# Attention from chunk 2 on in plain float32, the two heads of a unit in halves of the array

## The chip, the cores and the metric

The program runs on one core of one Trainium2 chip. A core has five engines that work at the same time, each in the order of its own instruction list, and that wait for each other by semaphores: TensorE (PE in the profile: matmuls, transposes by an identity; its weight loads are listed apart as PEld), VectorE (DVE), ScalarE (ACT), GpSimd (POOL) and SyncE (SP, which here issues DMAs). The metric is the device time of one execution in microseconds (us), as the median of several runs; lower is better.

## The reference

Three layers follow each other. The sizes are B, H, S, D = 4, 8, 576, 64 (so 2304 tokens of width 512), 2048 hidden columns in the second layer, and 8 experts with 1024 hidden columns in the third.

```python
scores = (q @ k.T) / sqrt(D)                       # per batch and head
scores = where((rel >= 0) & (rel < 128), scores - slope[h] * abs(rel), -1e9)
attn = exp(scores - max); attn = attn / (attn.sum(-1) + 1e-9)
x = attn @ v                                       # (2304, 512)
h = x @ w_in                                       # 2048 wide
x = (h * clip(h + 3, 0, 6) / 6) @ w_out
idx = argmax(cosine(x, expert_emb) / tau)          # one expert per token
out = gate * (relu(x @ w1[idx]) @ w2[idx])
```

A query sees its own key and the 127 before it, so a block of 128 queries needs at most two blocks of 128 keys.

## The kernel before

The 2304 tokens are nine chunks of 256 (c = 0 to 8). A chunk's attention is four **units** of two heads (p = 0 to 3). Chunks 0 and 1 use the class `Early`: loads of whole rows, transposes by PE, plain float32 matmuls, the two heads of a unit side by side in halves of the array (for the scores the upper and the lower 64 rows, for the values the left and the right 64 columns). Chunks 2 to 8 (28 units) use the class `Unit`. The batches end at token 576, 1152 and 1728, so the blocks differ by chunk: in chunks 3, 5 and 8 a unit has two query blocks of 128 with 256 keys each ("even"), in chunk 4 two blocks, one of them without keys before it, and in chunks 2, 6 and 7 three blocks, two of them of 64 queries.

`Unit` before works in float32r with every operand split into a rounded part and a remainder. `split_qk` (L570) casts the keys and the scaled queries on ACT and subtracts on DVE; two DMAs of ACT's queue (L591, L592) then exchange the two halves of the queries' tile into a second tile, q2. `split_v` (L594) splits the values on ACT or POOL. Each head has its own group of score matmuls (L625, two for each block, with all 128 rows), its own softmax (`soften`: DVE adds the table and takes the minimum, L639, joins own and earlier keys, L648 or L654, ACT makes the exponential, L659), `normalise` (DVE makes the reciprocal, L676 and L677, POOL or ACT multiplies, L680 to L690), transposes on PE (L697), `split_p` (ACT cast, DVE remainder by L160, POOL masks both parts, L711 and L715), value matmuls (L742, two for each window of keys), and `gather` (L753, L754), which adds the two halves of the result.

Chunks from 1 on go through the second layer in eight steps each: `gemm1` (L780, 24 matmuls into h_ps), `swish` (ACT relu L790, DVE gate L797), `split_g` (ACT cast gh, remainder gl on POOL or DVE by a table, I_GL), `gemm2` (L823, 12 matmuls into y_ps). `Route` chooses the experts of a finished chunk. The third layer comes after the last chunk.

What sets the order: for chunk 0 and the units of `Early` a planner lists the tasks (its ranks are PIECE_RANK, UNIT_RANK and so on). After it every call has a step number (`at`), and PE runs the calls in the order of these numbers; a step is about 3.7 us. UNITS_2 and UNIT say at which step a unit begins, PARTS the distances inside it, FIRST_1 and FIRST where the steps of the second layer stand. DVE, ACT, POOL and SP are ordered by the scheduler, which starts from the same calls. All PSUM tiles come from one pool of eight banks.

## Time and profile before

| what | value |
|---|---|
| runs | 845.07, 852.41, 852.37 us; median 852.37 us |
| the profiled execution | 850.65 us, its span from first to last instruction 848.9 us |
| PE busy | 809.2 us (95%) in 5404 matmuls |
| DVE, ACT, POOL busy | 551.0, 459.2, 314.5 us |
| mean granted TensorE clock | 0.968 of full speed |

The profile is of one execution. A timeline row gives the start, the length, the engine, the line, the tiles written and read, the shape and the number of merged instructions. The lengths of matmuls overlap, since they are pipelined; the time that PE really spends on a group is the distance from its start to the start of the next group. A plain float32 matmul appears as two instructions, a float32r matmul as one. "Idle before" in brackets is PE's wait and what ended it.

### The profile page before, as it was taken

The page shows a single profiled execution, that of the slowest core. Times are in us where ns is not written, and L with a number is a line of the kernel's source. Part 1 is how long each engine was busy: PE and PEld are TensorE (multiplying, and loading weights), DVE is VectorE, ACT ScalarE, POOL GpSimd, SP SyncE. Part 2 cuts the span into 40 slices and gives each one's busy share as a digit, 9 for nine tenths or more (in the row PEclk, how much of TensorE's full clock was granted, in tenths as well). Part 3 has the DMA queues.
Part 4 walks back from the last instruction along what each step waited for, and adds up shares of the span by engine and source line. Part 5 has one row for each costly group of instructions (what it writes and reads, how often), then busy time and mean ns, then how long its engine had stood idle before and what let it go on. Part 6 is the DMA issues. An engine that isn't in the chain of part 4 may idle for free. (4 is left out here: it accounts for less than half of the span.)

```text
span 848.9 us, 16092 instructions
## 1 busy us (share of the span) xinstructions
PE 809.2 (95%) x5404; PEld 721.3 (85%) x5404; DVE 551.0 (65%) x1482; ACT 459.2 (54%) x1140; POOL 314.5 (37%) x617
## 2 busy tenths in 40 slices
PE   5899989899999999999999999999999999999994
PEld 3666578679989999988899999998899999999993
DVE  4999967575767776867677776324565566447620
ACT  6676657466646566567467565333655445435410
POOL 1000014473544556776557645123233122132300
PEclk8699999899999999999999999999999999999997
DMA  9927133323333233233233221005647655465200
GB/s 263 332 81 221 79 69 67 44 58 80 58 56 83 47 65 81 52 58 72 43 58 86 50 48 29 2 25 165 221 133 239 226 182 197 169 217 177 100 24 26
DMA packets 156664, 90.86 MB, mean 107 GB/s; under 512 B 117491, under 2 KB 134003, under 8 KB 156576
## 3 DMA queue, kind: packets, MB, share of 16 engines
q1 hardware_dynamic: 148352, 72.85, 31.4%
q10 hardware_dynamic: 4480, 7.34, 4.0%
q0 software_dynamic: 3744, 9.58, 3.3%
q8 instruction: 45, 0.74, 0.4%
q14 instruction: 43, 0.35, 0.2%
HBM read 72.76 MB, written 9.74 MB: 97 GB/s over the span
## 5 line engine op out<-in xcount | busy, mean ns | idle before, releaser
L780 PE MATMUL h_ps<-xs,w_i 128*128 128x256 f32 x1536 | 202.3, 289 | 2.0 <-ACT xs L159 2.0
L780 PEld LDWEIGHTS h_ps<-xs,w_i 128*128 128x128 f32 x1536 | 192.1, 194 | 4.5 <-ACT xs L159 2.2
L823 PE MATMUL y_ps<-w_o,gh 128*128 128x512 f32 x512 | 167.0, 408 | 1.0 <-ACT gh L159 1.0
L823 PEld LDWEIGHTS y_ps<-w_o,gh 128*128 128x128 f32 x512 | 93.9, 193 | 18.8 <-ACT gh L159 1.3
L160 DVE TENSOR_TENSOR w_e<-st,w_e 128x1024 fp32r<-128x1024 f32 x64 | 77.4, 1233 | 47.8 <-ACT w_e L159 47.8
L1060 PE MATMUL ps_u<-x,w_e 128*128 128x280 f32 (+5 forms) x768 | 104.8, 293 | 0.0
L823 PE MATMUL y_ps<-w_o,gl 128*128 128x512 f32 x256 | 102.3, 400 | 1.4 <-POOL gl L160 1.4
L1060 PEld LDWEIGHTS ps_u<-x,w_e 128*128 128x128 f32 x768 | 100.0, 188 | 0.2
L797 DVE SCALAR_TENSOR_TENSOR u<-u,h_ps 128x512 f32<-128x512 f32 x72 | 49.2, 683 | 55.0 <-ACT u L790 54.7
L790 ACT ACTIVATE u<-h_ps,three 128x512 f32<-128x512 f32 x72 | 49.3, 684 | 65.4 <-PE h_ps L780 52.0
L659 ACT ACTIVATE pt<-pt,nm 128x128 f32<-128x128 f32 (+1 forms) x128 | 49.9, 391 | 61.9 <-DVE pt L648 24.8
L1084 PE MATMUL ps_o<-hs,w_e 128*128 128x280 f32 (+4 forms) x576 | 78.4, 295 | 0.0
L1084 PEld LDWEIGHTS ps_o<-hs,w_e 128*128 128x128 f32 x576 | 76.5, 188 | 0.0
L159 ACT CAST w_e<-st 128x1024 fp32r<-128x1024 f32 x64 | 65.3, 1049 | 15.4 <-DMA st<-in_moe_w_dram 6.0
L1159 POOL DMA_INDIRECT out_dram<-ob,ids x23 | 30.4, 1321 | 108.7 <-DVE ob L1158 99.4
L611 POOL TENSOR_TENSOR v<-vr,v 128x384 fp32r<-128x384 f32 (+4 forms) x48 | 35.6, 751 | 82.0 <-ACT v L608 79.8
L823 PEld LDWEIGHTS y_ps<-w_o,gl 128*128 128x128 f32 x256 | 49.1, 192 | 14.0 <-POOL gl L160 2.3
L159 ACT CAST gh<-u 128x512 fp32r<-128x512 f32 x64 | 39.6, 619 | 29.4 <-DVE u L797 28.8
L690 POOL TENSOR_TENSOR pt<-pt,rs 128x128 f32<-128x128 f32 (+2 forms) x80 | 33.6, 440 | 45.2 <-DVE rs L677 29.8
L1068 ACT ACTIVATE hs<-ps_u 128x280 fp32r<-128x280 f32 (+5 forms) x64 | 25.7, 404 | 45.3 <-PE ps_u L1060 44.0
L639 DVE CUSTOM_DVE_ANT_0 pt<-sc_ps,table 128x256 f32<-128x256 f32 (+3 forms) x128 | 44.1, 370 | 6.6 <-PE ps_pt L697 2.6
L1018 POOL DMA_INDIRECT xg<-ybuf,ids x20 | 22.9, 1145 | 55.8 <-DMA ids<-slots 41.9
(187 smaller groups left out, 1507.2 us busy)
## 6 DMA issues: line engine op xcount, KB each, us to landing
st<-in_moe_w_dram SPq DMA_DIRECT2D x32, 512.0 KB, 4.6
st<-in_moe_w_dram SPq DMA_DIRECT2D x16, 1024.0 KB, 8.9
wst<-in_moe_w_in_dram SPq DMA_DIRECT2D x8, 1024.0 KB, 8.6
wst<-in_moe_w_out_dram SPq DMA_DIRECT2D x8, 1024.0 KB, 8.6
q<-q ACTq DMA_DIRECT2D x56, 128.0 KB, 2.2
vr<-in_v_dram SPq DMA_DIRECT2D x72, 64.0 KB, 2.2
ybuf<-ys SPq DMA_DIRECT2D x18, 256.0 KB, 2.3
kr<-in_k_dram SPq DMA_DIRECT2D x48, 48.0 KB, 2.1
```

The lines of the kernel that those rows point to most:

```text
L159: nc.scalar.copy(hi, src)
L160: eng.tensor_tensor(out=lo, in0=src, in1=words(hi), op=ALU.subtract)
L611: either(I_VLO[self.c]).tensor_tensor(out=d[:, :, 1::2, :], in0=s, in1=words(d[:, :, 0::2, :]), op=ALU.subtract)
L639: V.tensor_tensor_reduce(out=pt[0:n, s0:s1], in0=self.sc_ps[0:n, s0:s1], in1=table[0:n, t0:t0 + c1 - c0], scale=-slope, scalar=3.0e38, op0 ...
L659: nc.scalar.activation(out=pt[0:n, a:a + m], in_=pt[0:n, a:a + m], func=AF.Exp, scale=-1.0, bias=nm[0:n, j:j + 1], accum_out=sm[0:n, j:j + 1],
L690: nc.gpsimd.tensor_tensor(out=w, in0=w, in1=rs[0:n, j:j + 1].to_broadcast([n, m]), op=ALU.mult)
L780: nc.tensor.matmul(hp[:, f, :], lhsT=w[:, a, kk, f * 128:(f + 1) * 128], rhs=xs[:, b, kk, :], start=(n == 0), stop=(n == 3 * KD - 1),)
L790: nc.scalar.activation(out=u, in_=hp, func=AF.Relu, bias=three, scale=1.0)
L797: V.scalar_tensor_tensor(out=u, in0=u, scalar=6.0, in1=h_t[c, i], op0=ALU.min, op1=ALU.mult)
L823: nc.tensor.matmul(y_t[c][t], lhsT=g[a][:, f, t * 128:(t + 1) * 128], rhs=w[:, b, f, :], start=(i == 0 and f == 0 and n == 0), stop=(i == ...
L1060: nc.tensor.matmul(ps, lhsT=w[:, a, kk, (f % 2) * 128:(f % 2) * 128 + 128], rhs=x[:, b, kk, c0:c1], start=(n == 0), stop=(n == 3 * KD - 1),)
L1084: nc.tensor.matmul(ps, lhsT=ws_t[j, 4 + f // 2][:, a, f % 2, d * 128:(d + 1) * 128], rhs=hs[:, b, f, 0:width(j)], start=(n == 0), stop=(n ...
```

## The change

`Unit` is written anew after the manner of `Early`. The keys and queries stay plain float32, and ACT only scales the queries (`scale`). The scores of both heads are issued as one group, head by head in the upper and lower half of the rows; `flip_p` transposes both heads into one bank; `values` runs both heads in the left and the right half of the columns into one bank, and the result needs no gathering. All splits, the exchange of q by DMA and half of POOL's masks are gone. `normalise` multiplies on DVE, and so are the remainders of x and of gl always made on DVE (the tables I_NORM to I_GL are gone). The step numbers of chunk 1, of the units and of `Route` are other ones, and raw tiles have more buffers.

```diff
-PIECE_RANK = (12.0, 3.38)
+PIECE_RANK = (12.0, 3.55)
-FIRST_1 = (0.0, 2.04, 3.99, 5.94, 7.89, 9.84, 11.79, 13.74)
-SECOND_1 = 2.95
+FIRST_1 = (0.01, 2.71, 4.66, 6.61, 8.56, 10.51, 12.46, 14.41)
+SECOND_1 = 3.34
-UNITS_2 = (0.3, 2.8, 5.3, 7.8)
-UNIT = (11.36, 3.6)
-PARTS = (
-    (2.28, 5.87, 8.0, 0.86, 1.01, 5.33, 5.0, 1.94),
-    (3.01, 6.0, 8.3, 0.91, 1.0, 4.93, 4.79, 1.0),
-)
-ROUTE = ((3.76, 4.57, 6, 8.04), (1, 1.43, 2.92, 4.5))
+UNITS_2 = (0.5, 3.2, 5.9, 8.6)
+UNIT = (13.87, 3.6)
+PARTS = ((1.5, 1.0, 3.6, 5.2, 5.0, 1.94), (1.5, 1.0, 3.6, 5.2, 4.79, 1.0))
+P_BUFS, V_BUFS = 3, 3
+ROUTE = ((3.76, 3.85, 6.05, 7.16), (1, 1.43, 2.92, 4.5))
-    raw = right.enter_context(tc.tile_pool(name="raw", bufs=1, side="right"))
-    at1 = right.enter_context(tc.tile_pool(name="at1", bufs=1, side="right"))
+    raw = right.enter_context(tc.tile_pool(name="raw", bufs=2, side="right"))
...
-        def split_qk(self):
...
-            nc.scalar.dma_start(out=words(q2)[0:64], in_=words(q1)[64:128])
-            nc.scalar.dma_start(out=words(q2)[64:128], in_=words(q1)[0:64])
-
-        def split_v(self):
...
+        def scale(self):
+            nc.scalar.activation(out=self.qT, in_=self.qT, func=AF.Copy, scale=units_of[:, self.p:self.p + 1])
...
+        def scores(self):
+            self.sc = [bank([128, 512], "sc_ps") for h in range(2)]
             for j, n, c0, cm, c1, s0, s1 in self.blocks():
+                for h in range(2):
+                    r = slice(64 * h, 64 * h + 64)
                     nc.tensor.matmul(
+                        self.sc[h][0:n, s0:s1], lhsT=self.qT[r, self.qoff[j]:self.qoff[j] + n], rhs=self.kT[r, c0:c1],
+                        start=True, stop=True,
+                    )
...
+                V.tensor_scalar(out=w, in0=w, scalar1=rs[0:n, j:j + 1], scalar2=None, op0=ALU.mult)
...
+        def unload_p(self, h):
+            self.pp[h] = pp = at2.tile([128, 512], F32, tag=("ph", "pl")[h], name="ph")
+            def part(o, p, src, n, r0, r1):
+                nc.scalar.copy(o, src)
...
+        def values(self):
             acc = bank([128, CH], "acc")
+            for x, (kj, kn, at, m, users) in enumerate(self.wins):
                 o, k0 = self.qoff[users[0]], self.row[kj]
+                for h in range(2):
                     nc.tensor.matmul(
+                        acc[64 * h:64 * h + 64, o:o + m], lhsT=self.vr[k0:k0 + kn, kj, 64 * h:64 * h + 64],
+                        rhs=self.pp[h][k0:k0 + kn, at:at + m],
+                        start=(x == 0), stop=(x == len(self.wins) - 1), skip_group_check=True,
+                    )
+            keep_x(self.c, self.p, acc, V)
...
-        split(gh, gl, g_t[c, i], either(not I_GL[c]))
+        split(gh, gl, g_t[c, i])
...
+        at(b, u.scale)
+        at(b + score, u.scores)
         for h in range(2):
+            at(b + score, u.soften, h)
+        for h in range(2):
+            at(b + score + norm, u.normalise, h)
+        at(b + flip, u.flip_p)
+        for h in range(2):
+            at(b + flip, u.unload_p, h)
+        at(b + value, u.values)
```

Three places show what the change does to the order. The first is PE in chunk 1's second layer, where the units of chunk 2 lie between its steps. Before, the transposes (ps_pt) and values (acc, from the rounded part ph and the remainder pl) of one head stand in one place and those of the other head elsewhere:

```order
L697 MATMUL ps_pt<-ident,pt 128x64
L697 MATMUL ps_pt<-ident,pt 128x128
L697 MATMUL ps_pt<-ident,pt 128x64
L742 MATMUL acc<-ph,v_1286 128x64
L742 MATMUL acc<-pl,v_1286 64x64
L742 MATMUL acc<-ph,v_1286 128x192
L742 MATMUL acc<-pl,v_1286 64x192
L742 MATMUL acc<-ph,v_1286 128x64
L742 MATMUL acc<-pl,v_1286 64x64
L742 MATMUL acc<-ph,v_1286 128x64
L742 MATMUL acc<-pl,v_1286 64x64
L780 MATMUL h_ps<-xs,w_i 128x256 x24
```

Now the transposes of both heads of a chunk 2 unit are one group, and one step later the scores of the next unit and the values of this one follow each other, each pair of rows being the two heads:

```order
L768 MATMUL ps_y<-ident,ys 128x128 x8
L631 MATMUL ps_pt<-ident,pt 128x64
L631 MATMUL ps_pt<-ident,pt 128x128
L631 MATMUL ps_pt<-ident,pt 128x64 x2
L631 MATMUL ps_pt<-ident,pt 128x128
L631 MATMUL ps_pt<-ident,pt 128x64
L697 MATMUL h_ps<-xs,w_i 128x256 x24
L569 MATMUL sc_ps<-kT,qT 64x192 x2
L569 MATMUL sc_ps<-kT,qT 128x128 x2
L569 MATMUL sc_ps<-kT,qT 64x192 x2
L671 MATMUL acc<-ph,vr 64x64 x2
L671 MATMUL acc<-ph,vr 64x192 x2
```

A unit has gone from six groups on PE (scores, transposes and values of each head) to three; the transposes cannot be finished before the second head's softmax is.

The second place is DVE in chunk 2's second layer, at an even unit of chunk 3. Before, it joins the keys (pt), makes the reciprocals (rs), and takes the transposes of the next unit's keys and queries between them; the multiplication is POOL's or ACT's:

```order
L648 TENSOR_TENSOR pt<-pt 128x2x128
L160 TENSOR_TENSOR gl<-u,gh 128x512
L676 TENSOR_SCALAR rs<-sums_131 128x2
L563 STREAM_TRANSPOSE kT<-kr 128x384
L677 RECIPROCAL rs<-rs 128x2
L563 STREAM_TRANSPOSE qT<-qr 128x256
L676 TENSOR_SCALAR rs<-sums_132 128x2
L677 RECIPROCAL rs<-rs 128x2
L754 TENSOR_TENSOR xa<-acc,xa 64x256 x2
L797 SCALAR_TENSOR_TENSOR u<-u,h_ps 128x512
L160 TENSOR_TENSOR pl<-ps_pt,ph 128x2x128
```

Now, behind the minima of the first head and the first block of the second, the same chain runs to the end on DVE before the gate of the second layer (u) comes:

```order
L582 ISA nm 128x1
L150 TENSOR_TENSOR xs<-acc,xs 128x256
L590 TENSOR_TENSOR pt<-pt 128x2x128
L618 TENSOR_SCALAR rs<-sums_128 128x2
L550 STREAM_TRANSPOSE kT<-kr 128x384
L619 RECIPROCAL rs<-rs 128x2
L550 STREAM_TRANSPOSE qT<-qr 128x256
L623 TENSOR_SCALAR pt<-pt,rs 128x128 x2
L618 TENSOR_SCALAR rs<-sums_129 128x2
L619 RECIPROCAL rs<-rs 128x2
L623 TENSOR_SCALAR pt<-pt,rs 128x128 x2
L714 SCALAR_TENSOR_TENSOR u<-u,h_ps 128x512
```

The multiplications (L623) have come to DVE and stand ahead of the gate; the gathering (xa), the remainder of the probabilities (pl) and the splits of keys and queries are gone from it.

The third place is ACT at the beginning of chunk 1's second layer. Before, the first unit of chunk 2 has its casts of keys and queries ahead of the square of the expert embedding (junk), and the DMAs of q beside the relu (u):

```order
L608 CAST v_1147<-vr 64x2x64
L579 CAST k_1018<-kT 64x384
L842 ACTIVATE ys<-y_ps 128x512
L579 CAST k_1018<-kT 64x384
L586 ACTIVATE q_1019<-qT 64x256 x2
L252 ACTIVATE junk,n_1037<-en 8x512
L591 DMA q_1020<-q_1019 64x512
L790 ACTIVATE u<-h_ps,three 128x512
L592 DMA q_1020<-q_1019 64x512
```

Now one scaling of the queries stands there:

```order
L759 ACTIVATE ys<-y_ps 128x512
L557 ACTIVATE qT<-qT,fixed 128x256
L759 ACTIVATE ys<-y_ps 128x512
L239 ACTIVATE junk,n_1022<-en 8x512
L707 ACTIVATE u<-h_ps,three 128x512
```

Three casts and one of two scalings have gone from ahead of the square, and no DMA of q is issued any more. PE's list up to the first step of chunk 1 is as before; DVE and ACT have a few of chunk 0's weight conversions in another order there.

## Rows read from the trace of the kernel before

**Rows 1.** The busy time of PE and of DVE over the whole span (page, part 1): us, share, instructions.

```profile
PE 809.2 (95%) x5404; PEld 721.3 (85%) x5404; DVE 551.0 (65%) x1482; ACT 459.2 (54%) x1140; POOL 314.5 (37%) x617
```

**Rows 2.** Busy time by stretch: the end of `Early` with chunk 0's second layer, chunk 1's second layer, that of chunks 2 to 7, and the last chunk's. Columns: stretch, its length, busy us (instructions) of PE, PEld, DVE, ACT and POOL, granted clock, DMA share, GB/s.

```profile
45.00:110.00 65.00, 61.37 (x282) 38.71 (x280) 64.02 (x121) 42.45 (x80) 0.40 (x1) 1.00 0.39 124
110.00:191.50 81.50, 74.16 (x463) 64.13 (x463) 55.89 (x203) 48.98 (x162) 39.04 (x110) 0.92 0.35 63
191.50:540.00 348.50, 345.85 (x2406) 316.33 (x2405) 249.55 (x812) 210.20 (x613) 196.08 (x409) 0.99 0.29 59
540.00:608.00 68.00, 65.51 (x422) 58.46 (x421) 27.44 (x61) 26.59 (x44) 16.67 (x14) 1.00 0.30 98
```

**Rows 3.** Whom PE waited for from 110 to 610 us: us in total, times, the longest.

```profile
PE sc_ps L625 <- DMA q<-q: 4.1, 1, 4.1
PE h_ps L780 <- ACT xs L159: 2.0, 1, 2.0
PE ps_en L259 <- DVE en L256: 1.9, 1, 1.9
PE y_ps L823 <- POOL gl L160: 1.4, 2, 0.9
PE acc L742 <- POOL pl L711: 1.3, 1, 1.3
PE y_ps L823 <- ACT gh L159: 1.0, 1, 1.0
PE acc L742 <- POOL pl L715: 0.6, 1, 0.6
```

**Rows 4.** Two stretches with a low clock, in the columns of rows 2: one behind the wait for the DMA of q, one behind the wait for xs.

```profile
158.00:164.70 6.70, 6.70 (x25) 5.48 (x26) 0.42 (x1) 0.37 (x1) 1.22 (x6) 0.59 0.27 45
252.00:256.00 4.00, 4.00 (x22) 3.87 (x21) 1.65 (x7) 1.71 (x4) 0.62 (x3) 0.57 0.22 35
```

**Rows 5.** Timeline of PE in the stretch of `Early`, where scores and values are already plain float32 in halves: a whole-array group (L770, eight matmuls of 256 columns), the values (L474) and the scores (L420) of chunk 1 units, and a whole-array group that no halves follow.

```profile
60.27 3.62 PE L770 MATMUL h_ps<-xf,w 128*128 128x256 f32 x16
63.81 1.09 PE L474 MATMUL acc<-ph,stage 128*64 128x128 f32 x12
64.83 1.13 PE L420 MATMUL sc_ps<-kt,qt 64*128 64x256 f32 x8
65.90 0.66 PE L400 MATMUL ps_qk<-ident,stage 128*128 128x128 f32 x4
...
90.64 3.62 PE L770 MATMUL h_ps<-xf,w 128*128 128x256 f32 x16
94.10 3.60 PE L814 MATMUL y_ps<-w,u 128*128 128x512 f32 x8
```

**Rows 6.** Timeline of PE around one head of an even unit: transposes, a gemm1, scores, the first of six value matmuls, the gemm2 behind them.

```profile
195.10 0.38 PE L697 MATMUL ps_pt<-ident,pt 128*128 128x128 f32 x2
195.23 3.11 PE L780 MATMUL h_ps<-xs,w_i 128*128 128x256 f32 x24
198.18 0.63 PE L625 MATMUL sc_ps<-k,q 128*128 128x256 f32 x4
198.65 0.22 PE L742 MATMUL acc<-ph,v 128*128 128x128 f32 x1
...
199.17 0.67 PE L823 MATMUL y_ps<-w_o,gh 128*128 128x512 f32 x2
```

**Rows 7.** The same around one head of chunk 2's units (three blocks): scores and what follows, then the first of eight value matmuls, the transposes of the next head, and what follows.

```profile
119.93 0.71 PE L625 MATMUL sc_ps<-k,q 128*64 128x192 f32 x6
120.47 0.64 PE L823 MATMUL y_ps<-w_o,gh 128*128 128x512 f32 x2
...
149.09 0.19 PE L742 MATMUL acc<-ph,v 128*128 128x64 f32 x1
...
149.90 0.73 PE L697 MATMUL ps_pt<-ident,pt 64*128 64x64 f32 x3
150.56 0.61 PE L780 MATMUL h_ps<-xs,w_i 128*128 128x256 f32 x3
```

**Rows 8.** Timeline of PE in the last chunk, with no attention beside it: a gemm1, and the first row of the gemm2 behind it; the gemm1 after that.

```profile
540.81 3.04 PE L780 MATMUL h_ps<-xs,w_i 128*128 128x256 f32 x24
543.68 0.63 PE L823 MATMUL y_ps<-w_o,gh 128*128 128x512 f32 x2
...
546.43 0.76 PE L780 MATMUL h_ps<-xs,w_i 128*128 128x256 f32 x5
```

**Rows 9.** Groups of DVE and ACT instructions by line and shape: count, busy us in total, mean ns of one, idle time before them and what ended it. L453 is the normalisation of `Early`, on DVE.

```profile
L639 DVE CUSTOM_DVE_ANT_0 pt<-sc_ps,table 128x256 f32<-128x256 f32 x72 | 29.3, 419 | 6.2 <-PE ps_pt L697 2.6 <-PE sc_ps L625 2.2 <-POOL pl L715 0.6
L639 DVE DVE_READ_ACCUMULATOR2_ANT nm<- 128x1 f32 x96 | 7.9, 82 | 0.0
L648 DVE TENSOR_TENSOR pt<-pt 128x256 f32<-128x256 f32 x24 | 12.4, 516 | 0.3
L676 DVE TENSOR_SCALAR rs<-sums 128x2 f32<-128x2 f32 x40 | 8.0, 200 | 11.7 <-ACT pt L659 11.5
L563 DVE STREAM_TRANSPOSE kT<-kr 128x384 f32<-128x384 f32 x24 | 13.7, 570 | 0.2
L453 DVE TENSOR_SCALAR pt<-pt,rs 128x128 f32<-128x128 f32 x8 | 2.3, 287 | 0.3
L659 ACT ACTIVATE pt<-pt,nm 128x128 f32<-128x128 f32 x96 | 37.9, 395 | 61.3 <-DVE pt L648 24.8 <-DVE pt L654 17.1 <-DVE nm L639 7.6
```

More of the change, by code (lines that the diff above doesn't have):

```diff
@@ L561, in turn @@
             def turn(src, width, nm):
-                t = at1.tile([128, width], F32, tag=nm, name=nm)
+                t = at2.tile([128, width], F32, tag=nm, name=nm)
                 V.transpose(out=t, in_=src.rearrange("p t i -> p (t i)")[:, 0:width])
@@ L662, in soften @@
                 )
-            self.pt[h], self.sm[h] = pt, sm
+            self.pt[h] = pt
         def joint(self, i):
@@ L672, in normalise @@
         def normalise(self, h):
-            pt, sm = self.pt[h], self.sm[h]
+            pt, sm = self.pt[h], sums[h]
             rs = at2.tile([128, 4], F32, tag="rs", name="rs")
@@ L677, in normalise @@
             V.reciprocal(out=rs[:, 0:nq], in_=rs[:, 0:nq])
-            if self.even and not I_NORM[self.c]:
-                w = pt.rearrange("p (j l k) -> p j l k", j=2, l=2)[:, :, 0, :]
-                nc.gpsimd.tensor_tensor(
-                    out=w, in0=w, in1=rs[:, 0:2, None].to_broadcast([128, 2, 128]), op=ALU.mult
-                )
-                return
             for j, n, *_ in self.blocks():
@@ new lines, in normalise, with flip_p @@
+                V.tensor_scalar(out=w, in0=w, scalar1=rs[0:n, j:j + 1], scalar2=None, op0=ALU.mult)
+        def flip_p(self):
+            self.ps_pt = bank([128, 2, CH], "ps_pt")
+            for h in range(2):
+                pt = self.pt[h]
+                for i, n, *_ in self.blocks():
+                    a, m = self.joint(i)
+                    nc.tensor.transpose(
+                        out=self.ps_pt[0:m, h, self.qoff[i]:self.qoff[i] + n], in_=pt[0:n, a:a + m],
+                        identity=ident[0:n, 0:n]
+                    )
@@ L726, in split_p @@
                 assert self.own[0] == 128 and self.prev[0] == 0
-                part(o, p, self.ps_pt.rearrange("p (j k) -> p j k", j=2), 2, 0, 128)
+                p, o = (pp.rearrange("p (j l k) -> p j l k", j=2, l=2)[:, :, l, :] for l in range(2))
+                part(o, p, ps.rearrange("p (j k) -> p j k", j=2), 2, 0, 128)
                 return
@@ L1286, in tile_kernel @@
         b = UNITS_2[n - n_early] if n < 12 else UNIT[0] + UNIT[1] * (n - 12)
-        score, flip, value, other, norm, vsplit, early, vearly = PARTS[min(u.c, 3) - 2]
+        score, norm, flip, value, early, vearly = PARTS[min(u.c, 3) - 2]
         if n >= AHEAD_UNITS:
@@ L1291, in tile_kernel @@
         at(b, u.transpose_qk)
-        at(b, u.split_qk)
-        at(b + value - vsplit, u.split_v)
+        at(b, u.scale)
+        at(b + score, u.scores)
         for h in range(2):
-            d = b + h * other
-            at(d + score, u.scores, h)
-            at(d + score, u.soften, h)
-            at(d + score + norm, u.normalise, h)
-            at(d + flip, u.flip_p, h)
-            at(d + flip, u.split_p, h)
-            at(d + value, u.values, h)
-            at(d + value, u.gather, h)
+            at(b + score, u.soften, h)
+        for h in range(2):
+            at(b + score + norm, u.normalise, h)
+        at(b + flip, u.flip_p)
+        for h in range(2):
+            at(b + flip, u.unload_p, h)
+        at(b + value, u.values)
         assert 0 < score < score + norm <= flip < value
-        assert b + value + other < begins(u.c)
-        assert b + value - vsplit > b - vearly
+        assert b + value < begins(u.c)
+        assert b + value > b - vearly
     for c in range(PLAIN_CHUNKS, NCH):
```

130 lines of the change are left out of this document (18 added, 112 removed).

## Prediction

> **What bounds the kernel now.** I read the busy times first. PE is busy for 809.2 of 848.9 us, DVE for 551.0 [rows 1], so work taken from DVE, ACT or POOL can pay only where PE waits for it. The stretches then say where PE is not busy or slow. Up to 110 us DVE is the limit (64.0 of 65.0 us) and PE waits for it; the change takes nothing from DVE there. From 110 to 191.5 us, where chunk 1's second layer runs with the units of chunk 2, PE is busy for 74.2 of 81.5 us at a clock of 0.92; from 191.5 to 540 us for 345.9 of 348.5 us at 0.99; behind that hardly any attention is left [rows 2]. The table of waits gives the names: of 12.3 us between 110 and 610 us the longest is 4.1 us for the DMA that exchanges q, then 2.0 for xs, 1.9 for the expert embedding, 1.4 and 1.0 for gl and gh, 1.9 for the remainder of the probabilities (pl) [rows 3]. What follows a wait is slow: behind the wait for q the granted clock is 0.59 (1.2 GHz instead of 2.4 for most of the stretch), behind that for xs 0.57 [rows 4]. So the stage is PE's own work, plus 12 us of waits, plus the price of the low clock: 81.5 x 0.08 + 348.5 x 0.01 = 10 us.
>
> **The change part by part.** Four terms, all on PE.
>
> First, PE's own work, from start to start. An even unit has scores of 0.47 (198.18 to 198.65), values of 0.52 and transposes of 0.13 us for each head [rows 6]: 2.24 us for both. Plain float32 is dearer: a whole-array group of eight matmuls of 256 columns takes 3.54 us [rows 5], 0.44 each, where 24 float32r ones take 2.87 [rows 8], 0.12 each. But the halves overlap. `Early` has the very shapes: scores of 4 matmuls of 256 columns (two heads, two blocks) take 1.07 us, where four whole-array ones would take 4 x 0.44 = 1.77; values of six matmuls with 1024 columns together take 1.02 [rows 5], where the same columns at that rate would take 1.77 too. The new even unit is 1.07 + 1.02 + 4 transposes at the present rate (0.26) = 2.35, so +0.1 us. Chunk 4 has fewer columns on both sides; I take it alike. 16 units: +2 us. A unit of three blocks (chunks 2, 6, 7) now has 0.54 for scores, 0.81 for values and 0.66 for transposes per head [rows 7]: 4.02. New: scores have 192 + 128 + 192 = 512 key columns, as the even unit: 1.07; values have 64 + 192 + 64 + 64 = 384 columns, 1.02 x 384 / 512 = 0.77; transposes stay 2 x 0.66 = 1.32. With a tenth more for the fourth window, 3.3 us: -0.7. If the 64-row windows gained nothing it would be 1.07 + 1.62 + 1.32 = 4.0, no gain. 12 units: -8 us, bounds 0 and -10. Last, a gemm1 takes 2.95 us ahead of attention [rows 6] and 2.87 without [rows 8]: each change between the layer and attention costs 0.08. A unit goes from six groups to three, so up to 3 x 0.08 x 28 = 7 us less; but a plain group ahead of the halves takes 3.54, and 3.46 where none follow [rows 5], so entering the halves costs as much, and some groups already stood side by side: -3, bounds 0 and -7. Sum of the term: **-9 us**.
>
> A rule speaks against this term. The Trainium skill (FP8 and Floating Point Precision, TensorE Precision Notes) has true float32 as four passes through the array; the 3.7 times between 0.44 and 0.12 agrees with it. By that rule alone, with the halves one after the other, the time would be that of the second rival below, 886 us; by the overlap of [rows 5] it is the sum's.
>
> Second, the waits. The one for q (4.1 us) cannot come back, since the DMA is gone. The two for pl (1.9) go with pl. That for gl (1.4) goes from POOL to DVE, which has 27.4 of 68 us to do there [rows 2]. That for gh (1.0) stays: it is ACT's. That for xs (2.0) had the gathering ahead of it; I let it go. That for the embedding (1.9): on ACT three casts and a scaling stood ahead of its square and one scaling of twice the height does now; I keep 0.6 of it. Together **-10.7 us**, bounds -4 (q alone) and -12.3.
>
> Third, the clock. 10 us by the sum above. Both stretches shown lie behind a wait that goes [rows 4]; but a new wait can lower the clock as an old one did, so I take 7 of 10 back: **-7 us**, bounds 0 and -10.
>
> Fourth, new waits. `normalise` now lies on DVE, the heads' transposes form one group, and both heads' chains must end ahead of it. In the steady order PE does between the scores of a unit and its transposes: the values of the unit before (1.02 [rows 5]), a gemm1 (2.95 [rows 6]), a gemm2 (546.43 - 543.68 = 2.75 [rows 8]): 6.7 us. DVE meanwhile does four additions of the table (0.42) and their reads (0.08), two joins (0.52), two additions to the row totals (0.20), the next unit's kT (0.57), four multiplications (0.29) [rows 9]: 5.2 us. The xs remainder, qT and two reciprocals stand between them in the order; as 0.42, 0.38 (two thirds of kT) and 2 x 0.20 they make 6.4. ACT's exponentials (0.40 each [rows 9]) run beside the other head's sums. So it just fits: 0.3 us of slack, and behind PE there is the gate of the step, which stands after the chain on DVE and is not late by it, because gemm2 of that step is a whole step later. Where the second head's exponentials come late (in `Route`'s steps, where ACT squares two tiles), or the slack is less (the first unit of chunk 3 has only a gemm1 and a gemm2 between, 5.7 us), PE waits: I put 0.5 us per chunk and 0.8 there, 4 us. In chunk 1's second layer it does not fit: a chunk 2 unit has three blocks per head with joins, gate and gl of two steps stand inside the chain, and between scores and transposes there lie 2.87 + 2.75 us and eight transposes. I put 1 to 1.5 us for each of four units: 5 us. Together **+9 us**; the bounds are 0 and the first rival.
>
> What it adds elsewhere hides: the moves of xs and gl to DVE lie under 346 us of PE work, of which DVE now uses 250 [rows 2] and loses the splits of k, q and pl. With this cover gone, it is the first rival. The new PIECE_RANK puts a few of DVE's conversions in another order in the stretch that DVE bounds; their number is the same: 0, bounds -1.5 and +1.5. The third layer comes as it did, only earlier.
>
> Sum: -9 - 10.7 - 7 + 9 = -17.7. From the profiled execution's own time, 850.65 us (1.75 more than its span; the median of the runs is 852.37, and one was 845.07), that is **833 us**.
>
> **The rivals.**
>
> The chain is late in every unit. DVE's list is in order: if the gate and gl of a step stand ahead of the multiplications in all units (two instructions on 128x512, at about 0.8 us each by the 0.42 of half that width), the chain is 8.0 us against 6.7, PE waits 1.3 us in 28 units, 36 us in place of 9, and the sum is -27 + 36 = +9: 860 us. It decides from 27 / 28 = 1.0 us per unit on. For it: DVE's row totals already have an idle time of 11.7 us in front, ended by ACT's exponentials [rows 9]. Against it: in chunk 2's steps the gate stands behind the chain.
>
> The halves do not overlap in these shapes. Blocks of 64 queries use a quarter of the array, which no row of `Early` shows. With nothing overlapped an even unit is 1.77 + 1.77 + 0.26 = 3.8 us, 1.56 more than before; over 28 units 44 us in place of the -9: 850.65 + 44 - 10.7 - 7 + 9 = 886 us. It needs the whole of it to be serial, which the 1.07 and 1.02 us of `Early` speak against.
>
> All waits and the low clock go and no new ones come: 850.65 - 9 - 12.3 - 10 = 819 us. Against it: the slack of 0.3 us.
>
> The gain is spent by halves: new waits of 0.6 us per unit and the clock as low as now: -20 + 17 = -3, 848 us. The low clock can come from new waits as from old ones.
>
> **How the numbers follow.** About 1% is what a measurement of this kernel can tell from no change: under 843.8 us is faster, over 860.9 slower, from the median. My forecast (823 to 843) has 0.50, the floor (under 823) 0.18, the spent gain (844 to 860) 0.19, the late chain 0.10, serial halves 0.03. So faster 0.68, same 0.19, slower 0.13. The range leaves out the slower cases and the lowest part of the floor: 817 to 853. The forecast's own range is 823 to 843.
>
> **What would show it.** In the new profile: PE's score group of an even unit at about 1.07 us and its values at 1.02 from start to start, the three-block unit at 3.3; no DMA of q and no wait for it; PE's waits in chunk 1's stretch under ps_pt, ended by DVE; chunk 1's second layer at some 73 us instead of 81.5; the stretch of chunks 2 to 7 at some 338 instead of 348.5. It is wrong if ps_pt waits for DVE by more than 20 us in total, if the score group of a pair takes over 1.5 us, or if the granted clock is low in new places for over 20 us.

## The result and the profile after

The changed kernel takes 824.96 us (median of 4 runs, 823.39 to 827.15), the kernel before 849.13 us in the runs beside it (845.07 to 852.41). The ratio is 0.9719, with a 95% interval of 0.9659 to 0.978. The profiled execution took 825.09 us (span 823.2), where the forecast was 833 and its range 817 to 853. Of the times further down, the medians of the kernel before with copied queries and of scores alone contain one slow run each (1305.53 and 4385.74 us), which no ratio contains.

The page's first part, for the whole span, as [rows 1]:

```profile
PE 793.2 (96%) x5404; PEld 687.0 (83%) x5404; DVE 465.6 (57%) x1363; ACT 388.8 (47%) x952; POOL 138.5 (17%) x272
```

The stretches that answer to [rows 2], in the same columns: from chunk 1's first gemm1 to chunk 2's first, from there to the last chunk's first, and the last chunk's.

```profile
109.00:172.50 63.50, 63.37 (x452) 51.11 (x451) 36.62 (x165) 32.03 (x111) 11.19 (x36) 1.00 0.32 53
172.50:525.60 353.10, 353.10 (x2494) 305.57 (x2493) 185.09 (x731) 160.55 (x482) 57.67 (x146) 1.00 0.21 41
525.60:581.20 55.60, 53.67 (x337) 47.85 (x335) 25.61 (x63) 23.03 (x36) 5.91 (x6) 0.97 0.34 115
```

And whom PE waited for from 109 to 590 us, as [rows 3]:

```profile
PE y_ps L740 <- ACT gh L149: 1.3, 1, 1.3
PE y_ps L740 <- DVE gl L150: 0.6, 1, 0.6
```

The reader is to see three things. From the first gemm1 of chunk 1 to the last gemm2 the kernel before takes 497.1 us (109.86 to 606.93 in its timeline) and the changed one 472.1 (109.10 to 581.19). That is 25.0 of the 25.6 us between the two profiled executions, so nothing that matters happened outside this stage. In the stage PE is busy from end to end; of 12.3 us of waits 1.9 are left. And nobody waits at ps_pt, where the forecast had put 9 us. The clock is 1.00 up to the last chunk.

The first two stretches cannot be set beside those of [rows 2] as they stand. Before, the last gemm2 of chunk 1 ends ahead of chunk 2's first gemm1:

```profile
191.29 0.39 PE L823 MATMUL y_ps<-w_o,gl 128*128 128x512 f32 x1
191.52 3.05 PE L780 MATMUL h_ps<-xs,w_i 128*128 128x256 f32 x24
```

In the changed kernel it comes behind it (y_ps at 175.74, below), and takes 2.85 us. With it counted to chunk 1 both times, chunk 1's second layer falls from 81.7 to 66.3 us, that of chunks 2 to 7 (before: to 552.05) from 360.5 to 350.2, and the last chunk's is 0.7 longer. So 15 of the 25 us lie where the units of chunk 2 run; 7.3 us of the waits and 6.2 us of low clock outside them lay there before.

PE's timeline around a unit of chunk 2 (scores at L569, the transposes of both heads at L631, values at L671; a plain float32 matmul is recorded as two, so x12 is six; a transpose is recorded as one):

```profile
120.07 1.03 PE L768 MATMUL ps_y<-ident,ys 128*128 128x128 f32 x8
121.04 1.26 PE L631 MATMUL ps_pt<-ident,pt 64*128 64x64 f32 x6
122.22 3.13 PE L697 MATMUL h_ps<-xs,w_i 128*128 128x256 f32 x24
125.28 1.44 PE L569 MATMUL sc_ps<-kT,qT 64*64 64x192 f32 x12
126.65 1.04 PE L671 MATMUL acc<-ph,vr 128*64 128x64 f32 x16
127.62 0.74 PE L740 MATMUL y_ps<-w_o,gh 128*128 128x512 f32 x2
```

and around even units, from the scores of one to its transposes, and the next one's scores:

```profile
168.55 1.13 PE L569 MATMUL sc_ps<-kT,qT 64*128 64x256 f32 x8
169.61 0.74 PE L740 MATMUL y_ps<-w_o,gh 128*128 128x512 f32 x2
...
172.51 3.04 PE L697 MATMUL h_ps<-xs,w_i 128*128 128x256 f32 x24
175.38 0.60 PE L631 MATMUL ps_pt<-ident,pt 128*128 128x128 f32 x4
175.74 0.71 PE L740 MATMUL y_ps<-w_o,gh 128*128 128x512 f32 x2
...
181.56 1.13 PE L569 MATMUL sc_ps<-kT,qT 64*128 64x256 f32 x8
182.62 1.09 PE L671 MATMUL acc<-ph,vr 128*64 128x128 f32 x12
183.64 0.73 PE L740 MATMUL y_ps<-w_o,gh 128*128 128x512 f32 x2
```

Start to start, the even unit costs 1.06 + 1.02 + 0.36 = 2.44 us (forecast 2.35, before 2.24) and the unit of chunk 2 costs 1.37 + 0.97 + 1.18 = 3.52 (forecast 3.3, before 4.02).

DVE in that first even unit, from its first addition of the table to the second head's multiplications:

```profile
170.04 0.42 DVE L582 CUSTOM_DVE_ANT_0 pt<-sc_ps,table 128x256 f32<-128x256 f32 x1
170.38 0.08 DVE L582 DVE_READ_ACCUMULATOR2_ANT nm<- 128x1 f32 x1
170.38 0.42 DVE L582 CUSTOM_DVE_ANT_0 pt<-sc_ps,table 128x256 f32<-128x256 f32 x1
...
173.30 0.48 DVE L623 TENSOR_SCALAR pt<-pt,rs 128x128 f32<-128x128 f32 x2
173.70 0.57 DVE L550 STREAM_TRANSPOSE kT<-kr 128x384 f32<-128x384 f32 x1
...
174.55 0.49 DVE L623 TENSOR_SCALAR pt<-pt,rs 128x128 f32<-128x128 f32 x2
```

The chain ends at 175.04, 0.34 us ahead of the transposes at 175.38. Note the pace: an addition is printed with 0.42 us, but the next one starts 0.34 us after it, the read between them included. The Trainium skill (Perfetto Trace Analysis, Per-instruction lifecycle) says that a DVE instruction's printed end is the acknowledgement of its write, while the next may begin to fetch when it has finished executing; the overlap here agrees with that.

In the first unit of chunk 2, PE's scores and the transposes' neighbours, and on DVE the first addition of the table and the second head's multiplications:

```profile
112.97 1.44 PE L569 MATMUL sc_ps<-kT,qT 64*64 64x192 f32 x12
114.34 3.14 PE L697 MATMUL h_ps<-xs,w_i 128*128 128x256 f32 x24
```

```profile
114.44 0.35 DVE L582 CUSTOM_DVE_ANT_0 pt<-sc_ps,table 64x192 f32<-64x192 f32 x1 [0.46 <-PE sc_ps L569]
...
119.52 0.67 DVE L623 TENSOR_SCALAR pt<-pt,rs 64x128 f32<-64x128 f32 x3
```

The chain ends at 120.19, 0.85 us ahead of that unit's transposes at 121.04. Taken in the same way for all 28 units, the time between the last multiplication's end and the transposes' start is 0.34 to 7.39 us, with a median near 1.6; only 6 units have under 0.9.

### The profile page after: what moved, and what is told of

It reads as the page before. It is cut to its first block, busy times and chain, and to the rows that moved or that the text cites. A ratio compares the mean times of both kernels' runs of the same rounds, so it can differ in the third digit from the quotient of the medians.

```text
span 823.2 us, 15002 instructions
## 1 busy us (share of the span) xinstructions
PE 793.2 (96%) x5404; PEld 687.0 (83%) x5404; DVE 465.6 (57%) x1363; ACT 388.8 (47%) x952; POOL 138.5 (17%) x272
## 3 DMA queue, kind: packets, MB, share of 16 engines
q1 hardware_dynamic: 148352, 72.85, 32.5%
## 5 line engine op out<-in xcount | busy, mean ns | idle before, releaser
L697 PE MATMUL h_ps<-xs,w_i 128*128 128x256 f32 x1536 | 198.3, 285 | 0.0
L740 PE MATMUL y_ps<-w_o,gh 128*128 128x512 f32 x512 | 163.8, 401 | 1.3 <-ACT gh L149 1.3
L740 PEld LDWEIGHTS y_ps<-w_o,gh 128*128 128x128 f32 x512 | 92.0, 189 | 20.5 <-issue 1.6
L644 POOL TENSOR_SCALAR_AFFINE_SELECT ph<-ph 128x256 f32<-128x256 f32 (+3 forms) x80 | 25.6, 334 | 240.6 <-ACT ph L641 232.9
L150 DVE TENSOR_TENSOR gl<-u,gh 128x512 fp32r<-128x512 f32 x64 | 45.7, 715 | 30.1 <-ACT gh L149 30.1
L986 DVE SCALAR_TENSOR_TENSOR hs<-ps_u,hs 128x280 fp32r<-128x280 f32 (+5 forms) x64 | 27.9, 443 | 20.0 <-ACT hs L985 20.0
```

The costliest lines, as they stand in the source:

```text
L150: eng.tensor_tensor(out=lo, in0=src, in1=words(hi), op=ALU.subtract)
L697: nc.tensor.matmul(hp[:, f, :], lhsT=w[:, a, kk, f * 128:(f + 1) * 128], rhs=xs[:, b, kk, :], start=(n == 0), stop=(n == 3 * KD - 1),)
L740: nc.tensor.matmul(y_t[c][t], lhsT=g[a][:, f, t * 128:(t + 1) * 128], rhs=w[:, b, f, :], start=(i == 0 and f == 0 and n == 0), stop=(i == ...
L986: V.scalar_tensor_tensor(out=hs[:, 1, f, c0:c1], in0=ps, scalar=0.0, in1=words(hs[:, 0, f, c0:c1]), op0=ALU.max, op1=ALU.subtract)
```

## The experiments

My theory after the result: the first three terms of the sum were right, and the fourth is nothing because the chain ahead of the transposes is shorter than I had counted. The rivals: the halves' price has another cause than overlap; the clock or the waits did more than the sum says; the step numbers or the move of the multiplications did it. Each kernel was timed beside runs of the kernel before; what counts is the ratio.

**Heads one after the other.**

```diff
-            for j, n, c0, cm, c1, s0, s1 in self.blocks():
-                for h in range(2):
-                    r = slice(64 * h, 64 * h + 64)
+            for h in range(2):
+                r = slice(64 * h, 64 * h + 64)
+                for j, n, c0, cm, c1, s0, s1 in self.blocks():
...
-            for x, (kj, kn, at, m, users) in enumerate(self.wins):
+            for h in range(2):
+                for x, (kj, kn, at, m, users) in enumerate(self.wins):
```

> The changed kernel with the scores and the values of a unit written head after head (all matmuls of the first head, then all of the second) instead of by turns; the work is the same. Theory (two heads overlap because neighbours in the list lie in different halves of the array): a pair's scores go from 1.06 to about 1.7 us and its values from 1.02 to about 1.6, less in units of three blocks (some 0.75 us for both together), so 16 x 1.3 + 12 x 0.75 = about 30 us, 850 to 860 us, with PE busy and no new waits. Rival (the time of a plain float32 group does not depend on which half the neighbour is in, and 1.06 us is simply what these shapes cost): 825 us, scores still at 1.06.

848.32 us, 1.0033 (1.0007 to 1.0058) of the kernel before: the whole gain is gone. PE's timeline, for a unit of chunk 2, then the scores of an even unit, then the values of one:

```profile
126.95 2.30 PE L569 MATMUL sc_ps<-kT,qT 64*64 64x192 f32 x12
129.18 1.98 PE L671 MATMUL acc<-ph,vr 128*64 128x64 f32 x16
131.10 0.73 PE L740 MATMUL y_ps<-w_o,gh 128*128 128x512 f32 x2
...
176.49 1.14 PE L569 MATMUL sc_ps<-kT,qT 64*128 64x256 f32 x8
177.56 0.74 PE L740 MATMUL y_ps<-w_o,gh 128*128 128x512 f32 x2
...
190.54 1.36 PE L671 MATMUL acc<-ph,vr 128*64 128x128 f32 x12
191.83 0.73 PE L740 MATMUL y_ps<-w_o,gh 128*128 128x512 f32 x2
```

In chunk 2 the scores go from 1.37 to 2.23 us and the values from 0.97 to 1.92; an even unit's values from 1.02 to 1.29. Over the stage the score groups go from 30.4 to 38.7 us and the values from 28.3 to 45.1, together 25.1 us, and nothing else on PE changes by more than 2 us. Overlap is what pays. But an even unit's scores take 1.07 us, as by turns, so there the order by turns is not what makes it: a surprise for the theory, and the reason for the next kernel.

**One head's scores alone.**

```diff
-            self.sc = [bank([128, 512], "sc_ps") for h in range(2)]
+            self.sc = [bank([128, 512], "sc_ps")] * 2
...
-                for h in range(2):
+                for h in range(1):
```

> The changed kernel with the scores of the first head only; the second head's softening reads the first head's scores, so its probabilities are not its own. It asks what one half of the array costs alone: with both heads an even unit's scores take 1.06 us, in turns as well as head after head. Theory (a matmul in one half costs as much as one in the whole array, 0.44 us for 256 columns, and neighbours in the other half run beside it even a place apart in the list): two matmuls in one half, 0.85 to 0.95 us, hardly less than four in both. Rival (a matmul of half height is simply cheaper, 0.27 us, and nothing overlaps): 0.5 to 0.55 us.

(Its whole time, 1081 us, tells nothing, since other probabilities send other rows to the experts. The stage of attention can be read.) PE's timeline for the same two kinds of unit:

```profile
124.39 1.42 PE L569 MATMUL sc_ps<-kT,qT 64*64 64x192 f32 x6
125.74 1.04 PE L671 MATMUL acc<-ph,vr 128*64 128x64 f32 x16
...
167.92 1.13 PE L569 MATMUL sc_ps<-kT,qT 64*128 64x256 f32 x4
168.97 0.74 PE L740 MATMUL y_ps<-w_o,gh 128*128 128x512 f32 x2
```

Half the matmuls take 1.05 us where all took 1.06, and 1.35 where all took 1.37. A lone half is a little slower than the 0.85 to 0.95 that I had (why, I did not trace), and the second head's scores are free: in all 28 units the lone head takes what both take, within 0.02 us. So the scores of even units overlap fully in either order; the rival of a cheaper matmul is out. The Trainium skill (TensorEngine Tiling (Array Packing), Key Properties) has tiles of the array run independently of each other; these two kernels agree.

**Sorted by the shape in the array.** The same section of the Trainium skill (TensorEngine Tiling (Array Packing), Key Properties) says that a change of the tiling mode drains TensorE. That would explain why the scores lost by the order of heads only in the units with blocks of 64 queries: in them the shape changes between neighbours (64*64, 64*128, 64*64). It would not explain the 0.27 us that the values of even units lost, whose shape does not change; that stays open.

```diff
-            for j, n, c0, cm, c1, s0, s1 in self.blocks():
+            for j, n, c0, cm, c1, s0, s1 in sorted(self.blocks(), key=lambda x: x[1]):
...
-            for h in range(2):
-                pt = self.pt[h]
-                for i, n, *_ in self.blocks():
+            for i, n, *_ in sorted(self.blocks(), key=lambda x: (x[1], self.joint(x[0])[1])):
+                for h in range(2):
+                    pt = self.pt[h]
...
-            for x, (kj, kn, at, m, users) in enumerate(self.wins):
+            for x, (kj, kn, at, m, users) in enumerate(sorted(self.wins, key=lambda x: x[1])):
```

> The changed kernel with the matmuls of a unit sorted by the shape they take of the array, those of 64 queries first: scores, transposes (heads by turns within a shape) and values; the work is the same, and even units keep their order but for the transposes' heads. In a unit of three blocks six transposes take 1.18 us, four in an even unit 0.36. Theory (a change of the array's shape between two matmuls costs time): the six transposes fall to 0.6 to 0.9 us and the scores of 1.37 to 1.2 or less, 0.4 to 0.7 us in 8 units, 3 to 6 us in all, against the changed kernel on the same chip. Rival (a transpose of 64 queries costs that by itself): no change.

> The changed kernel as it is, beside the others on the same chip, for the comparison with the order by shape: 0.97 to 0.98 of the kernel before.

819.78 us (6 runs, 817.99 to 823.32) against 822.91 (821.36 to 824.71) for the changed kernel beside it; 0.9703 (0.9659 to 0.9747) and 0.9734 (0.9692 to 0.9777) of the kernel before. The two intervals overlap, but five of the six runs lie below the other kernel's lowest, and in the traces, with the clock at 1.00 in both, the stage is 465.4 us against 469.9. The transposes' groups (16.3 to 12.2 us) and the scores' (30.4 to 29.8) make that difference. PE's timeline of the sorted kernel, chunk 2:

```profile
120.40 0.83 PE L631 MATMUL ps_pt<-ident,pt 64*128 64x64 f32 x6
120.98 3.11 PE L697 MATMUL h_ps<-xs,w_i 128*128 128x256 f32 x24
124.03 1.29 PE L569 MATMUL sc_ps<-kT,qT 64*64 64x192 f32 x12
125.25 1.09 PE L671 MATMUL acc<-ph,vr 64*64 64x64 f32 x16
```

Six transposes take 0.58 us where they took 1.18, the scores 1.22 where they took 1.37. A change of shape between neighbours costs, which agrees with that section of the Trainium skill; a 64-query transpose as such does not cost it. The values stay at 28.3 us in all. In chunk 6, where the order by block already has the 64-query blocks side by side, the scores take 1.22 us in both kernels, and even units, where only the heads' order changes, stay as they were.

**More multiplications ahead of the transposes.** (With `range(1)` and with `range(3)`.)

```diff
                 V.tensor_scalar(out=w, in0=w, scalar1=rs[0:n, j:j + 1], scalar2=None, op0=ALU.mult)
+                for _ in range(1):
+                    V.tensor_scalar(out=w, in0=w, scalar1=1.0, scalar2=None, op0=ALU.mult)
```

> The changed kernel with one more multiplication on DVE (by 1.0) behind each one that normalises: 4 of about 0.23 us in an even unit and 6 in one of three blocks, 0.9 to 1.4 us more in the chain ahead of the transposes. The trace of the changed kernel has, between the end of the second head's last multiplication and the start of the transposes, 0.35 to 7.4 us, with a median of 1.5 us. Theory (the slack is what this trace shows): about ten units wait, 0.1 to 0.6 us each, together 3 us, so 826 to 830 us, waits at ps_pt ended by DVE. Rival (the slack is 0.3 us in every unit, as the sum of the forecast had it): 28 x 0.7 = 20 us, about 845 us.

> The same with three more multiplications behind each: 2.8 us more in the chain of an even unit, 4.2 us in one of three blocks. Theory (the slack is what the trace shows): chunk 2's units wait 2 to 3.4 us each and most others 0.8 to 2.5, together about 45 us, 860 to 880 us, the waits at ps_pt ended by DVE; the granted clock falls in some of the stretches behind these waits. Rival for the clock (PE's granted clock does not follow its waits): the waits come, and the clock stays at 0.98.

One more: 823.8 us, 0.9753 (0.9702 to 0.9805), not to be told from the changed kernel; PE waits 0.3 us at ps_pt, once. Slack of 0.3 us everywhere is refuted, and my list of slacks was even too careful. Three more: 845.42 us, 0.9998 (0.9979 to 1.0017), all of the gain spent, though I had expected 860 to 880. Whom PE waited for, and two of its stretches:

```profile
PE ps_pt L633 <- DVE pt L625: 10.9, 17, 1.2
```

```profile
100.00:170.00 70.00, 64.91 (x414) 49.00 (x414) 50.42 (x233) 33.31 (x110) 11.16 (x36) 0.95 0.30 51
...
310.00:380.00 70.00, 65.78 (x437) 55.80 (x436) 40.94 (x197) 29.13 (x92) 11.66 (x31) 0.95 0.21 41
```

The transposes' groups take 32.5 us in all where they took 16.3, and gemm1 and gemm2, whose work is the same, 382.0 instead of 374.7 (sums from start to start over the stage). (Of the 16.2 us, 10.9 are the waits listed; the rest lies between the transposes without a listed wait.) Those 7.3 us are the clock: it falls to 0.95 in the stretches where PE waits most, chunk 2's and chunk 6's units. Together that is 23.5 of the 23.7 us by which the stage is longer (495.8 for 472.1). The rival for the clock is out. Why the waits came to half of what I had subtracted, unit by unit, I did not trace; a unit that waits leaves DVE time to get ahead with its other work.

**The DMA of the queries put back, and taken out of the kernel before.**

```diff
             nc.scalar.activation(out=self.qT, in_=self.qT, func=AF.Copy, scale=units_of[:, self.p:self.p + 1])
+            qd = at2.tile([128, CH], F32, tag="qd", bufs=1, name="qd")
+            nc.scalar.dma_start(out=qd[0:64], in_=self.qT[0:64])
+            nc.scalar.dma_start(out=qd[64:128], in_=self.qT[64:128])
+            self.qT = qd
```

> The changed kernel with a DMA put back on the way of the queries: after the scaling two transfers (64 partitions each, issued by ACT) bring the scaled queries into another tile that the scores read. Theory (a wait of PE for such a DMA comes only where little time lies between the scaling and the scores; in the changed kernel that is 2.5 to 3.6 us in six units of chunk 2 and the start of chunk 3, and over 5 us behind): waits of 1 to 5 us in all before 195 us and none behind, a stretch or two at the low clock after them, 827 to 834 us. Rival (such a transfer is a cost everywhere, by ACT's queue or by traffic): waits at the scores in all chunks, over 835 us. If nothing comes back (825), the DMA's wait in the kernel before belonged to its own order and not to the DMA.

832.83 us, 0.9849 (0.9801 to 0.9897). Two waits in chunk 1's second layer, then the two stretches:

```profile
PE sc_ps L573 <- DMA qd<-qT: 3.6, 1, 3.6
PE ps_en L246 <- DVE en L243: 0.9, 1, 0.9
```

```profile
108.00:178.00 70.00, 65.51 (x451) 52.66 (x450) 36.16 (x163) 32.10 (x111) 11.07 (x36) 0.95 0.35 58
178.00:532.00 354.00, 353.82 (x2497) 305.98 (x2496) 186.49 (x731) 159.73 (x482) 57.62 (x146) 1.00 0.24 50
```

Chunk 1's second layer, cut as in the changed kernel, goes from 63.4 to 70 us: 3.6 of wait for the DMA, 0.9 of wait for the embedding, and 2.7 of low clock outside the waits (0.05 of 70 us is 3.5, but part of it lies in the wait for the DMA). Chunks 2 to 7 take 354 us against 353. The rest of the difference lies in the last chunk, where the wait for gh is 3.0 us in place of 1.3; that chunk has no scores, and differs by 2 us between two profiles of the changed kernel too. A DMA in front of the scores costs where little lies between, once as a wait and again by the clock; no other scores wait for it.

```diff
-            nc.scalar.dma_start(out=words(q2)[0:64], in_=words(q1)[64:128])
-            nc.scalar.dma_start(out=words(q2)[64:128], in_=words(q1)[0:64])
+            V.tensor_copy(out=q2[0:64], in_=words(q1)[64:128])
+            V.tensor_copy(out=q2[64:128], in_=words(q1)[0:64])
```

> The kernel before, with the exchange of the scaled queries' two halves made by two copies on DVE instead of two DMAs; all else as it was, float32r passes, splits and gathering. Theory (the wait of 4.1 us for that DMA and the low clock behind it are a cost of their own, whatever number format the attention has): the wait goes, the stretch behind it runs at full clock (2.7 us by its 0.59 in 6.7 us), 6 to 7 us less than before. Rival (what is late there is late anyway, by DVE or ACT, and the DMA was only the last to come): within 2 us of before, with a wait at the same scores under another name.

843.7 us, 0.9953 (0.9922 to 0.9984): about 4 us, between the two theories. The wait for q is gone; the longest of PE's waits, and chunk 1's stretch, are now

```profile
PE ps_en L259 <- DVE en L256: 2.8, 1, 2.8
```

```profile
110.00:188.00 78.00, 73.66 (x464) 63.74 (x463) 60.15 (x211) 47.85 (x158) 39.96 (x110) 0.93 0.23 44
```

so the stretch is 3.6 us shorter (78.0 for 81.6), but the embedding is later than the 1.9 us of [rows 3], and the clock stays low there. Removing one wait of several leaves the others to lower the clock.

**One half of the change alone.** On the kernel before, with its step numbers: first only `scale` and `scores` as changed, then only `values` and `unload_p` as changed.

```diff
-        at(b, u.split_qk)
+        at(b, u.scale)
...
             for j, n, c0, cm, c1, s0, s1 in self.blocks():
-                for a, qq in enumerate((self.q1, self.q2)):
+                for h in range(2):
```

> The kernel before with the scores alone changed: plain float32 with both heads by turns in halves, one scaling of the queries, no splits of keys and queries, no DMA of the queries; probabilities, values, gathering and all step numbers as before. Theory (on PE the scores win nothing: their groups take 34.5 us in the kernel before, 4.1 of it the wait for the DMA, and 30.4 in the changed one; what they bring is that wait and the low clock behind it): the sum of the score groups 30 to 31 us, about 4 to 8 us less than before in all, 838 to 842 us. Rival (the scores bring most of the gain, since the splits of keys and queries fall away on ACT and DVE): 830 us or less.

```diff
-        at(b + value - vsplit, u.split_v)
...
-                for src, r in zip(self.pp[h], (128, 64)):
+                for h in range(2):
...
-            at(d + value, u.gather, h)
```

> The kernel before with the values alone changed: plain float32 with both heads by turns in halves, at the step of the second head; no splits of values and probabilities, no gathering; scores with their splits and DMA, transposes per head and normalising as before. Theory (the values hold PE's own gain: their groups take 40.5 us in the kernel before, 1.9 of it waits for pl, and 28.3 in the changed one): the sum of the groups at acc 28 to 30 us, 11 to 15 us less than before in all, 831 to 835 us, the wait for the DMA of q still there. Rival (the values in the changed kernel gain only together with the scores): under 6 us less.

Scores alone: 838.29 us, 0.9916 (0.9881 to 0.995); their groups take 30.4 us, as in the changed kernel, and no wait for q is left. Values alone: 829.43 us, 0.9805 (0.9748 to 0.9862), somewhat better than I had said; the groups at acc take 28.3 us where they took 40.5, and the DMA is still waited for:

```profile
PE sc_ps L604 <- DMA q<-q: 2.6, 1, 2.6
```

The product of the two ratios, 0.9916 x 0.9805 = 0.9723, is the ratio of the whole change (0.9719, again 0.9734). The two halves of the change add up, and the rest of it (joined transposes, multiplications on DVE, new step numbers) brings nothing beyond them that these intervals, of some 6 us, can show.

**Of the rest, two parts undone in the changed kernel.** (The joined transposes and the deeper buffers were not undone.) The multiplications on POOL:

```diff
-                V.tensor_scalar(out=w, in0=w, scalar1=rs[0:n, j:j + 1], scalar2=None, op0=ALU.mult)
+                nc.gpsimd.tensor_tensor(out=w, in0=w, in1=rs[0:n, j:j + 1].to_broadcast([n, m]), op=ALU.mult)
```

> The changed kernel with the normalising multiplications on POOL, where the kernel before had most of them (0.44 us each there against 0.28 on DVE), in place of DVE. Theory (the chain's length ahead of the transposes is what counts): four or six multiplications at 0.16 us more and a hop from DVE to POOL, about 1 us longer, so the units with under 1 us of slack wait, 3 to 8 us in all, 827 to 833 us. Rival (DVE's list is what is short, and each unit gains what DVE no longer does): within 2 us of 825 or below, without waits at the transposes.

824.61 us, 0.9761 (0.9739 to 0.9784): no change, as the rival had it. The slacks shrink by about 0.3 us (median 1.34 us, the even unit above to 0.02), and no transposes wait.

The step numbers of the kernel before:

```diff
-SECOND_1 = 3.34
+SECOND_1 = 2.95
...
-UNITS_2 = (0.5, 3.2, 5.9, 8.6)
-UNIT = (13.87, 3.6)
+UNITS_2 = (0.3, 2.8, 5.3, 7.8)
+UNIT = (11.36, 3.6)
```

> The changed kernel with the step numbers of the kernel before for the loads of the pieces, the units of chunk 1 and 2, the start of the later units and the routing (they come earlier and closer together); the steps inside a unit stay as changed. Theory (the slack of a unit comes from what PE does between its scores and its transposes, and the numbers are there to place units where that is enough): units of chunk 2 stand 2.5 instead of 2.7 steps apart and wait for the chain, 2 to 8 us more than the changed kernel, most of it before 200 us. Rival (any spread does, since PE has other work at each step): within 2 us of 825.

829.21 us, 0.9825 (0.9797 to 0.9853): by the times 4 to 6 us more than the changed kernel, by the ratios 8 to 9, and 4.6 us more than POOL's multiplications (824.61) on the same chip. The size is as expected and the place is not: no unit waits for the chain, and nothing waits before 200 us. PE waits for POOL's masks in a unit whose transposes stand too close to its values:

```profile
400.94 0.65 PE L671 MATMUL acc<-ph,vr 128*64 128x256 f32 x2 [2.04 <-POOL ph L648]
402.21 1.23 PE L671 MATMUL acc<-ph,vr 128*64 128x256 f32 x10 [0.62 <-POOL ph L648]
```

Those 2.7 us are most of the 3.5 us by which the stage is longer (475.6 for 472.1); what remains is not traced.

## Why the prediction was right, and where it was off

The time lies in the range and on the forecast's side, but 8 us below the number. By its own terms, for the stage (clock and work are summed over PE's time outside the waits, matmul by matmul, with the granted clock of the trace; work is what that time comes to at full clock):

| term | forecast, us | measured, us | from |
|---|---|---|---|
| PE's own work | -9 | -4.9 | 473.4 to 468.5 |
| waits that go | -10.7 | -10.5 | 12.4 (12.3 by the rounded [rows 3]) to 1.9 |
| clock | -7 | -9.6 | 11.3 to 1.7 |
| new waits | +9 | 0 | no wait at ps_pt |
| sum | -17.7 | -25 | 497.1 to 472.1 |

The 8 us are thus a difference of two errors: nearly 12 us too little from new waits and clock, 4 us too much from PE's own work. That the number came this near is in part luck.

**PE's own work** was right in its mechanism: scores 1.06 (1.07 said) and values 1.02 (1.02 said) in even units. Units of three blocks are 0.2 us dearer than said in chunk 2 (3.52): I took the scores by their columns, 1.07, and they take 1.37, in part for the changes of shape, as the sorted kernel shows with 1.22. In chunk 6 they cost 3.3, as said. That the halves overlap, which carried the term against the rule weighed in the prediction, is shown by the heads one after the other and by the lone head. The gain lies in the values (37.7 to 28.3 us at full clock); the scores win nothing on PE (30.4 us for 34.5 with 4.1 of wait), they take away the DMA. Two things were wrong in the sum. Chunk 7 does not have three blocks: its units have two of 128 queries, the first with 64 earlier keys, as the x40 of L676 with two columns in [rows 9] shows (two heads of 20 units). So there are 8 units of three blocks and 20 others, and by the forecast's own rates the units gain 4 us, not 6. Measured, the units' three groups gain 7.3 us at full clock. And the 3 us for fewer changes between layer and attention did not come: all other groups of PE together take 2.4 us more at full clock.

**The waits** went one by one as listed: q, xs, pl and the embedding wholly, gl to 0.6, gh still there (1.3). That for the embedding, of which I had kept 0.6, has no row any more.

**The clock** came back with the waits, more than the 7 that I took, since no new wait lowers it up to the last chunk. The 10 us that I had put on it, from clocks of two digits, were 11.3. That a wait costs more than itself, by the clock behind it, is shown by three more multiplications (7.3 us on 16.2) and by the DMA put back (2.7 on 3.6 and 0.9 of waits).

**New waits** is the step that failed: +9 forecast, 0 measured. The time that PE has was read rightly, and DVE's chain was taken too long. In the steady order the working said 6.7 us for PE and 6.4 for the chain, so that it "just fits: 0.3 us of slack". The unit whose scores stand at 181.56 is of that kind: PE has 6.8 us (182.62 to 189.39), of which the gate takes the first 0.4, and the chain takes 5.1 us, with gl and the xs remainder in it, and leaves 1.3. I had added printed durations, where the pace is shorter, and counted qT, which stands behind the chain. For the first unit of chunk 3 the working had 5.7 us and a wait of 0.8. PE has 5.8 us there (169.61 to 175.38), the gate takes the first 0.4, and the chain runs in 5.0 (170.04 to 175.04), with gl in it: no wait, and 0.34 us of slack. In chunk 2, where I said 1 to 1.5 us of wait, DVE starts as the scores end (114.44 and 114.34), and its chain of 5.75 us fits into the 6.7 us that PE has until 121.04, with one gate and one gl inside. One more multiplication behind each, which the slack of 0.3 could not have held, cost nothing.

What happened is the rival "all waits and the low clock go and no new ones come", to which I had given 0.18 for the sake of that slack. Its 819 us are 6 below the measured time: PE's own gain is 4 us smaller, and 1.9 us of waits stayed. Of the other rivals, a chain that is late in every unit and halves that do not overlap are both refuted in this kernel, and both were made to happen: three more multiplications and the heads one after the other each spend the whole gain.

Of the signs named, chunk 1's second layer is 66.3 us like for like (73 said). The second layer of chunks 2 to 7 has no like in my 338, which ended at 540 us of before and not at the chunk's end: there 10.5 us were said to go, and 10.3 went (360.5 to 350.2). So the forecast missed in chunk 1's second layer, where it had put 5 us of new waits and where most of the low clock lay.

## What to carry to other kernels

Add up a chain on an engine from start to start, since printed durations of neighbours overlap (0.42 us printed, 0.34 us of pace here), and look unit by unit at what really stands between its ends. Count a wait of PE one and a half times to twice where the clock falls behind it, and expect that back only when the neighbouring waits are gone too. When matmuls share the array by halves, keep equal shapes next to each other before you look for fewer or cheaper matmuls.

## What the runs showed of the hardware

- In even units the second head's scores are free, even if they are not the neighbours of the first head's in the list: four plain float32 matmuls of 256 columns in two halves take 1.06 us by turns, 1.07 head after head, and two of them alone 1.05.
- Changes of shape are not small: six transposes take 1.18 us with 64 and 128 queries by turns and 0.58 us sorted (chunk 2).
- A DMA of 128 KB from SBUF to SBUF has a median of 2.2 us from issue to landing in the kernel before, but at the one wait of 4.1 us the scores begin 7.9 us after the second transfer's issue (150.02 to 157.92 in the trace of before).
- POOL's multiplications take 0.40 us where DVE's take 0.28 and run at a pace of 0.2, and it makes no difference to the time, since the chain has that slack.
